# Whole-head loads of keys and values, and one load of the query weights, for the first element of a two-layer decode step

## The chip, the cores and the metric

The kernel runs on one core of one Trainium2 chip. The metric is the device time of one execution in microseconds, lower is better. The core has a matrix engine (PE; its weight loads are listed as PEld), a vector engine (DVE), an activation engine (ACT), a general engine (POOL), and a queue engine (SP) that issues nearly all transfers from the chip's memory. The transfers run on 16 DMA engines.

## What is computed

The reference is two passes of the same layer over four single-token elements (B = 4). In each pass an element attends over its cache and then goes through a gated feed-forward part. The caches and the weights are the same in both passes.

```python
def attention(x, k_cache, v_cache, wq, wo):        # x: 4 x 1 x 512
    q = (x @ wq).reshape(4, 1, 32, 128)            # 32 query heads
    k = repeat(k_cache, 4, axis=1)                 # caches: 4 x 8 heads x 4096 x 128
    v = repeat(v_cache, 4, axis=1)
    scores = einsum("bhqd,bhkd->bhqk", q, k) * 128 ** -0.5
    o = einsum("bhqk,bhkd->bhqd", softmax(scores), v)
    return o.reshape(4, 1, 4096) @ wo
def ffn(x, w_gate, w_up, w_down):                  # 512 -> 1792 -> 512
    return (gelu(x @ w_gate) * (x @ w_up)) @ w_down

for _ in range(2):
    x = x + attention(layernorm(x), k_cache, v_cache, wq, wo)
    x = x + ffn(layernorm(x), w_gate, w_up, w_down)
```

Everything is bf16. Since a softmax sum doesn't depend on the order of its 4096 positions, positions may be spread over partitions in any way, if keys and values of an element are spread alike.

## The kernel before

**Tiles.** The cache of one head is 4096 positions of 128 numbers, 1 MB. It is handled as two tiles (t = 0 and 1) of 512 KB: 128 partitions, and in each 16 positions one behind the other, which is 4 KB in a row. The 8 heads fall into two groups of 4, called `gx` and `gy`, so a group has 8 tiles of keys and 8 of values. Keys have room for 16 tiles (`KP`), one element's whole cache; values have a ring of 8 tiles (`slots`, `VRing`).

**One element's attention.** For a group, `q_first` (L921) projects the queries with `wq` (64 small matmuls on PE at L252) and corrects them for the layernorm on DVE (L923, L926, L248, L249). `q_build` spreads them into block weights `qb` (PE L324, DVE L331). Each key tile is turned in place by DVE (`turn`, L507, a stream transpose of 32x32 blocks). Then PE multiplies a turned tile with `qb` in 4 matmuls (`scores_of`, L557). The four heads of a group write to different groups of 32 output partitions, so that matmuls of different heads can run beside each other, while those of one head follow each other. `soft` takes the maximum (DVE L567), then the exponential (ACT L579); `soft_turn` (DVE L587), `soft_swap` (PE L609, ACT L612) and `soft_den`/`soft_recip` (PE L592, DVE L597) bring the probabilities into place. `vals.step(n)` then takes n value tiles, 16 matmuls each (PE L805); it ends with a scaling on DVE (L642) for each pair of heads that is complete. A value tile's place in the ring is free when its matmuls have run, and `ring.pump` then issues the next load into it.

**What sets the order.** The schedule is written out by hand: every engine takes its instructions in the order in which the program issues them. All large loads go through the one SP queue in program order. Up to eight loads are in flight; the ninth waits until the first has landed.

**The first element** (`attend_first`, L899 and on) has no earlier work to hide behind. SP issues, in this order: the half of `wq` that belongs to `gx` (2 MB), 8 key tiles of `gx`, the other half of `wq` (2 MB), 8 key tiles of `gy`, 8 value tiles of `gx`, 8 value tiles of `gy` (each into the place of a `gx` tile that has been used), and then the weights `wo`, `wg`, `wu`, `wd` (`load_rest`, L145 to L153), and the next element's keys. Keys are turned and scored by halves: all four heads at t = 0, then all four at t = 1.

Of the kernel before, what the change touches and what calls it, by code (L numbers as in the profile page):

```python
# [9 lines left out]
BF16 = mybir.dt.bfloat16  # L10
# [5 lines left out]
P = 128  # L16
# [8 lines left out]
GH = 4  # L25
CH = 16
V_SLOTS = 8
# [7 lines left out]
def kernel(  # L35
# [15 lines left out]
    _, Hkv, Sk, Dh = A_k_cache.shape  # L51
# [5 lines left out]
    KD = D // P  # L57
    KF = F // P
    C = Sk // P
    NT = C // CH  # L60
    assert NT == 2 and CH * QS == 512
    NG = Hkv // GH
    assert NG == 2
    HG = GH * rep
    NK = GH * BE
    W = 4 * QD
    TG = GH * NT
# [3 lines left out]
    wts = ctx.enter_context(tc.tile_pool(name="wts", bufs=1))  # L71
# [14 lines left out]

    dq = nc.sync

    wq_sb = [wts.tile([P, KD, HG * Dh], BF16, name=f"wq_sb{g}") for g in range(NG)]
    wo_sb = wts.tile([P, Hq, D], BF16, name="wo_sb")  # L90
    wg_sb = wts.tile([P, KD, F], BF16, name="wg_sb")
    wu_sb = wts.tile([P, KD, F], BF16, name="wu_sb")
    wd_sb = wts.tile([P, KF, D], BF16, name="wd_sb")
    KP = [[[wts.tile([P, 2, CH, Dh], BF16, name=f"kp{g}_{t}_{j}") for j in range(GH // 2)]
           for t in range(NT)] for g in range(NG)]
    slots = [wts.tile([P, CH, Dh], BF16, name=f"v_t{i}") for i in range(V_SLOTS)]
    wq_dram = A_wq.rearrange("(k p) n -> p k n", p=P)
    wo_dram = A_wo.rearrange("(i p) n -> p i n", p=P)

# [14 lines left out]
    qb = const.tile([P, W + NK * 2 * W], BF16, name="qb")  # L114
    cs_f = const.tile([P, 2, KF], FP32, name="cs_f")

    place = {(g * GH + s, t): (KP[g][t][s // 2], s % 2)
             for g in range(NG) for s in range(GH) for t in range(NT)}

    def k_tile(i, t):  # L120
        pair, n = place[i, t]
        return pair[:, n]

    def acc(shape, name, t=None):
        if t is None:
# [10 lines left out]
        return v.unsqueeze(1).broadcast_to([P, WIDE // n, n])  # L136

    def cache_tile(cache, b, kvh, t):
        return cache[b, kvh].rearrange("(t p c) d -> t p c d", t=NT, p=P)[t]

    def load_wq(g):
        n = HG * Dh
        dq.dma_start(out=wq_sb[g][:], in_=wq_dram[:, :, g * n:(g + 1) * n])

    def load_rest():  # L145
        n = Hq // 4
# [67 lines left out]
    class Norm:  # L214


        def __init__(self, st):
            ln = small.tile([P, 3, B], FP32, name="ln", tag="ln")
            self.mean, self.up, self.down = ln[:, 0, 1:2], ln[:, 1, 1:2], ln[:, 2, 1:2]
            self.ss, self.var, self.msq = ln[:, 0, :1], ln[:, 1, :1], ln[:, 2, :1]  # L220
            nc.vector.tensor_copy(out=ln[:, 0, :2], in_=st[:, 0])
# [33 lines left out]
    def q_proj(rhs, nb, g):  # L255
        w = nb if nb > 1 else WIDE
        q = acc([HG, w], "q")
        q_heads(q, rhs, nb, g, range(HG))
        return q
# [213 lines left out]
    class Keys:  # L473
# [4 lines left out]

        def tile(self, n):
            g, u = divmod(n, TG)  # L480
            t, s = divmod(u, GH)
            return self.groups[g] * GH + s, t

        def load(self, count):
            for _ in range(count):
                kvh, t = self.tile(self.nl)
                self.nl += 1
                dq.dma_start(out=k_tile(kvh, t), in_=cache_tile(A_k_cache, self.b, kvh, t))

        def load_pairs(self, count):  # L490
            for _ in range(count):
                kvh, t = self.tile(self.nl)
                (to, n), (other, m) = place[kvh, t], place[kvh + 1, t]
                if to is not other or (n, m) != (0, 1):
                    self.load(2)
                    continue
                self.nl += 2
                pair = A_k_cache[self.b, kvh:kvh + 2].rearrange("h (t p c) d -> t p h c d",
                                                                t=NT, p=P)
                dq.dma_start(out=to[:], in_=pair[t])  # L500

        def turn(self, count=1):
            for _ in range(count):
# [40 lines left out]
    singly = tuple((s,) for s in range(GH))  # L544
    last_alone = (tuple(range(GH - 1)), (GH - 1,))

    def scores(sc, g, t, runs=together):
        for run in runs:
            scores_of(sc, g, [(s, t) for s in run])

    def scores_of(sc, g, run):
        for be in range(BE):
            for s, t in run:
                n = s * BE + be
                w0 = n * 2 * W + (W if t == 0 else 0)
                kt = k_tile(g * GH + s, t).rearrange("p c (b j e) -> p c b j e", b=NB, e=2)
                nc.tensor.matmul(sc[s * QS:(s + 1) * QS], lhsT=qb[:, w0:w0 + 2 * W],  # L557
                                 rhs=kt[:, :, be // 2, :, be % 2],
                                 start=(t == 0 and be == 0),
                                 stop=(t == NT - 1 and be == BE - 1))  # L560
# [59 lines left out]
    def one(b):  # L620
        return [(g * GH + s, t) for g in first_groups[b] for s in range(GH) for t in range(NT)]

    def two(b):

        order = one(b)
        kept = order[len(order) - keep[b]:]
        rest = [u for u in reversed(order[:TG * (NG - 1)])]
        own = [u for u in reversed(order[TG * (NG - 1):]) if u not in kept]
        apart = [own.pop() for _ in range(2 if b else 0)][::-1]
        other = order[:TG]  # L630
        assert len(rest) == len(other)
        return list(reversed(kept)), own, other, apart
# [11 lines left out]
    class VRing:  # L644


        def __init__(self):
            self.free = [v[:] for v in slots]
            self.seq, self.at, self.ready = [], 0, {}

        def extend(self, layer, b, tiles):
# [2 lines left out]
        def pump(self, spare=None):  # L654
            free = self.free if spare is None else spare
            while self.at < len(self.seq) and free:
                key = self.seq[self.at]
                self.at += 1
                v = free.pop(0)
                dq.dma_start(out=v, in_=cache_tile(A_v_cache, *key[1:]))  # L660
                self.ready[key] = (v, spare is None)
# [214 lines left out]
    def dst1(b):  # L876
        last = one(b)[-1][0]
        return lambda k, n: (OL_bf[:] if k == last else OT_bf[:, k * rep:(k + n) * rep])
# [20 lines left out]
    def attend_first():  # L899

        b, (gx, gy) = 0, first_groups[0]
        prob1 = {}
        keys = Keys(b, (gx, gy))
        kept, own, other, _ = two(b)
        vals = Values(1, b, one(b), prob1, dst1(b), keeps=kept)
        ring.extend(1, b, one(b))
        load_wq(gx)
        keys.load(TG)
        load_wq(gy)
        keys.load(TG)  # L910
        ring.pump()
        make_identity(nc, ident_bf[:])
        build_consts()
        xT_ps = ps_sm.tile([P, KD, B], BF16, name="xT_ps", tag="sm")
        for k in range(KD):
            nc.tensor.transpose(xT_ps[:, k, :], x_bf[:B, k * P:(k + 1) * P], ident_bf[:B, :B])
        nc.vector.tensor_copy(out=xb[:, :, :B], in_=xT_ps[:])
        nc.vector.tensor_copy(out=XX.rearrange("p b k -> p k b"), in_=xT_ps[:])
        rstd1, mr1 = ln_scale(B, stats(0, B))

        def q_first(g):  # L921
            q = q_proj(lambda k: xb[:, k, :B + 1], B + 1, g)
            nc.vector.tensor_scalar(out=cs_q[:, g], in0=q[:, :, B], scalar1=float(D), scalar2=None,  # L923
                                    op0=ALU.mult)
            t = apart(wd_sb, [HG, B])
            nc.vector.tensor_tensor(out=t, in0=cols(cs_q[:, g], HG, B),  # L926
                                    in1=rows(mr1, HG, B), op=ALU.mult)
            center(q1_bf[:, g], q[:, :, :B], t, rstd1, B)

        q_first(gx)  # L930
        q_build(q1_bf[:, gx, :, b])
        keys.turn(4)
        sc1 = new_scores()
        scores(sc1, gx, 0, singly)
        keys.turn(4)
        scores(sc1, gx, 1, singly)
        p0 = soft(sc1)
        q_first(gy)
        soft_turn(p0)
        q_build(q1_bf[:, gy, :, b])  # L940
        pe, den = soft_swap(p0), soft_den(p0)
        keys.turn()
        prob1[gx] = (pe, soft_recip(den))
        keys.turn(3)
        vals.step(2)
        sc1 = new_scores()
        scores(sc1, gy, 0, last_alone)
        keys.turn(4)
        vals.step(3)
        scores(sc1, gy, 1, last_alone)  # L950
        vals.step(3)
        p0 = soft(sc1)
        soft_turn(p0)
        prob1[gy] = (soft_swap(p0), soft_recip(soft_den(p0)))
        vals.step(TG)
        assert vals.left() == 0
        load_rest()
        scr = Scratch()
        early = Early(b + 1, second_groups[b])
        proj = OutProj(o1(b), 1)  # L960
        for n, h in enumerate(pairs(one(b))):
            if n:
                busy(WARM, proj.bank[:, KD * WIDE:KD * WIDE + QS], ident_bf, start=False)
            proj.heads(h, hp)
        ring.extend(2, b, own)
        return proj.y, early, scr
# [391 lines left out]
    for b in range(B):  # L1358
        y = dense(b, y, prev, Scratch()) if b else dense_first(y, scr)
        gx, gy = second_groups[b]  # L1360
# [87 lines left out]
```

## Time and profile before

| | us |
|---|---|
| median of 3 runs | 270.62 (269.87 to 271.5) |
| the profiled execution, its own time | 273.38 |
| its span, first to last instruction | 271.6 |
| mean granted PE clock | 0.827 of full speed |
| DMA: moved 103.08 MB, mean over the span | 380 GB/s |
| busy: PE / DVE / ACT / POOL | 193.3 / 177.2 / 63.4 / 3.9 |
| chain that ended last: DMA / DVE / PE | 44% / 23% / 19% |

The page gives busy time by engine, a strip of 40 equal slices of the span, the chain of work that ended last (followed back from the last instruction to whatever released it), and the costliest groups of instructions. Queries of the trace give single instructions in order of time: start and duration in us, engine, line, operation, what is written and read, and in brackets how long the engine had stood idle and what ended that. Times count from the start of the span. The profiled execution's own time is 1.78 us longer than its span.

### The profile page before, as it was taken

What the parts mean: (1) busy time and instruction counts of PE and PEld (TensorE: products, weight loads), DVE (VectorE), ACT (ScalarE), POOL (GpSimd) and SP (SyncE); (2) the same over time, 40 slices, a digit from 0 to 9 for tenths busy, and PEclk for the clock granted to TensorE, in tenths of its full rate; (3) what the DMA queues carried; (4) which work ended last, traced back from release to release, by engine and by line L of the source; (5) the groups of instructions that cost most, each with busy time, mean ns of one, the idle gap of its engine ahead of it and who ended that gap; (6) DMA issues with size and microseconds to landing.
All of it is one profiled execution on the core that took longest, in us unless ns stands there. A gap on an engine that the chain in (4) does not pass through costs nothing.

```text
span 271.6 us, 9070 instructions
## 1 busy us (share of the span) xinstructions
PE 193.3 (71%) x4020; PEld 117.2 (43%) x4023; DVE 177.2 (65%) x435; ACT 63.4 (23%) x124; POOL 3.9 (1%) x10
## 2 busy tenths in 40 slices
PE   1395264655699796888769869587699685788783
PEld 1333133554475644445426245354372453443551
DVE  3493952151136999776748998756679987369843
ACT  1001001100405202024115320332144203164610
POOL 2000000000001000000000000000000000000010
PEclk9997559555599777959989989959989899599987
DMA  7999999999997999999999999999999999999910
GB/s 256 419 417 421 417 421 417 408 383 406 405 383 276 407 417 419 419 403 358 375 416 419 419 417 417 417 419 372 363 417 417 417 422 415 417 346 392 412 41 1
DMA packets 32574, 103.08 MB, mean 380 GB/s; under 512 B 2836, under 2 KB 8728, under 8 KB 32536
## 3 DMA queue, kind: packets, MB, share of 16 engines
q1 hardware_dynamic: 32512, 102.51, 95.0%
q8 instruction: 31, 0.51, 0.7%
q14 instruction: 7, 0.06, 0.0%
q10 hardware_dynamic: 24, 0.01, 0.0%
HBM read 102.50 MB, written 0.00 MB: 377 GB/s over the span
## 4 chain that ended last, share of the span: by engine, by line
DMA 44%; DVE 23%; PE 19%; SPq 9%; issue 3%; ACT 2%; DVEq 0%
DMA v_t<-in_A_v_cache_dram 19%; DMA kp<-in_A_k_cache_dram 17%; DVE kp L507 12%; PE sc L557 5%; DMA kp<-in_A_v_cache_dram 5%; SPq L148 4%; DMA wd_sb<-in_B_w_down_dram 4%; SPq L153 3%; PE ot L805 2%; PE so L738 2%; PE q L280 2%; DVE pe L587 1%; PE g L280 1%; PE y L252 1%; DVE q L286 1%
## 5 line engine op out<-in xcount | busy, mean ns | idle before, releaser
L507 DVE STREAM_TRANSPOSE kp<-kp 128x1024 f32<-128x1024 f32 x64 | 74.0, 1208 | 0.0
L557 PE MATMUL sc<-kp,qb 128*32 128x512 bf16 x512 | 66.2, 449 | 6.2 <-DVE kp L507 2.1
L805 PE MATMUL ot<-pe,v_t 128*128 128x32 bf16 x1120 | 35.5, 181 | 15.1 <-DMA v_t<-in_A_v_cache_dram 12.2
L805 PEld LDWEIGHTS <-v_t 128*128 128x128 bf16 x1120 | 33.0, 100 | 24.6 <-DMA v_t<-in_A_v_cache_dram 15.5
L557 PEld LDWEIGHTS <-qb 128*32 128x32 bf16 x512 | 22.3, 103 | 40.4 <-issue 23.0
L579 ACT ACTIVATE pe<-sc,nl 128x512 bf16<-128x512 f32 x8 | 5.5, 687 | 84.8 <-DVE pe L576 67.1
L609 PE MATMUL x<-pe,ident_bf 128*32 128x128 bf16 x192 | 5.6, 243 | 15.2 <-DVE pe L587 15.1
L746 DVE STREAM_TRANSPOSE so<-so 128x256 f32<-128x256 f32 (+1 forms) x19 | 11.1, 584 | 3.8 <-PE so L738 3.8
L609 PEld LDWEIGHTS <-ident_bf 128*32 128x32 bf16 x256 | 5.6, 106 | 18.4 <-issue 16.4
L738 PE MATMUL so<-v_t,pe 128*32 128x256 bf16 x192 | 9.3, 312 | 4.2 <-DMA v_t<-in_A_v_cache_dram 2.0
L567 DVE TENSOR_REDUCE pe<-sc 128x1 f32<-128x512 f32 x12 | 8.3, 690 | 6.0 <-PE sc L557 5.9
L252 PEld LDWEIGHTS <-wo_sb 128*128 128x128 bf16 x256 | 8.7, 104 | 6.3 <-DMA wo_sb<-in_A_wo_dram 5.4
L612 ACT CAST pe<-x 128x512 bf16<-128x512 f32 x12 | 7.0, 586 | 18.5 <-PE x L609 18.5
L738 PE MATMUL so<-v_t,pl 128*32 128x256 bf16 x192 | 9.9, 299 | 1.6 <-DMA v_t<-in_A_v_cache_dram 1.6
L252 PE MATMUL y<-OT_bf,wo_sb 128*128 128x32 bf16 x192 | 7.3, 190 | 5.1 <-DMA wo_sb<-in_A_wo_dram 4.9
L642 DVE TENSOR_TENSOR OT_bf<-ot,rden 128x8 bf16<-128x8 f32 (+1 forms) x20 | 3.0, 156 | 12.1 <-PE ot L805 12.0
L324 PE MATMUL qe<-q_bf,ident_bf 128*32 128x16 bf16 (+1 forms) x272 | 5.5, 175 | 7.6 <-DVE q_bf L306 4.8
L252 PE MATMUL q<-xb,wq_sb 128*128 128x5 bf16 (+1 forms) x192 | 5.7, 170 | 7.3 <-DMA wq_sb<-in_A_wq_dram 7.3
L587 DVE STREAM_TRANSPOSE pe<-pe 128x512 bf16<-128x512 bf16 x12 | 8.4, 699 | 3.4 <-ACT pe L579 3.4
L395 DVE TENSOR_TENSOR xb<-XX,y 128x4 bf16<-128x4 f32 (+1 forms) x9 | 1.6, 173 | 12.9 <-PE y L252 12.8
L376 PE MATMUL yr<-wo_sb,OT_bf 128*2 128x512 bf16 (+1 forms) x96 | 9.4, 453 | 0.0
L738 PEld LDWEIGHTS <-pe 128*32 128x32 bf16 x208 | 5.4, 105 | 9.0 <-issue 3.1
(153 smaller groups left out, 241.0 us busy)
## 6 DMA issues: line engine op xcount, KB each, us to landing
v_t<-in_A_v_cache_dram SPq DMA_DIRECT2D x97, 512.0 KB, 8.1
kp<-in_A_k_cache_dram SPq DMA_DIRECT2D x56, 512.0 KB, 10.0
wq_sb<-in_A_wq_dram SPq DMA_DIRECT2D x2, 2048.0 KB
wo_sb<-in_A_wo_dram SPq DMA_DIRECT2D x4, 1024.0 KB, 11.4
kp<-in_A_k_cache_dram SPq DMA_DIRECT2D x4, 1024.0 KB, 8.8
wq_sb<-in_A_v_cache_dram SPq DMA_DIRECT2D x3, 1024.0 KB, 12.7
wg_sb<-in_B_w_gate_dram SPq DMA_DIRECT2D x1, 1792.0 KB, 12.4
wu_sb<-in_B_w_up_dram SPq DMA_DIRECT2D x1, 1792.0 KB
```

The costliest lines, as they stand in the source:

```text
L148: dq.dma_start(out=wo_sb[:, i * n:(i + 1) * n], in_=wo_dram[:, i * n:(i + 1) * n])
L153: dq.dma_start(out=wd_sb[:, lo:hi], in_=wd_dram[:, lo:hi])
L252: nc.tensor.matmul(dst, lhsT=lhsT, rhs=rhs, start=first, stop=last, skip_group_check=True)
L376: nc.tensor.matmul(self.rows[j:j + x.shape[1]], lhsT=x, rhs=wo_sb[:, i], start=self.n < QD, stop=True, skip_group_check=True)
L507: nc.vector.transpose(out=words, in_=words)
L557: nc.tensor.matmul(sc[s * QS:(s + 1) * QS], lhsT=qb[:, w0:w0 + 2 * W], rhs=kt[:, :, be // 2, :, be % 2], start=(t == 0 and be == 0), stop= ...
L567: nc.vector.tensor_reduce(out=m, in_=sc.rearrange("p c j -> p (c j)"), axis=AX.X, op=ALU.min if norm else ALU.max)
L587: nc.vector.transpose(out=flat, in_=flat)
L609: nc.tensor.matmul(x[a * QS:(a + 1) * QS, s], lhsT=ident_bf[:, s * QS:(s + 1) * QS], rhs=pT[:, a], start=True, stop=True, skip_group_check ...
L738: nc.tensor.matmul(ps[d, :NW * QS], lhsT=x[:, w:w + NW].rearrange("p c h -> p (c h)"), rhs=v[:, i:i + NW, d], start=first and i == 0, stop ...
L746: nc.vector.transpose(out=flat, in_=flat)
L805: nc.tensor.matmul(self.ot[:, s % 2], lhsT=v[:, i, :], rhs=wide(pe[:, s, t * CH + i, :]), start=(done == 0 and i == 0), stop=(done == NT - ...
```

## The change

It touches the first element alone. A head's two tiles now lie beside each other, and which position goes to which partition is changed for the element's keys and values: a partition holds 32 positions in a row (8 KB) instead of two runs of 16 (4 KB each). So a head's keys, or its layer-1 values, come with one load of 1 MB. `wq` comes with one load of 4 MB, issued after the keys of two heads. Keys are turned, and scored, head by head. In group `gy` three heads are turned and scored together, then come 3 value tiles, and then the fourth head. The second pass's values of this element are still loaded by tiles of 4 KB rows, now 8 KB apart. Loads of the other elements keep their form.

```diff
-    wq_sb = [wts.tile([P, KD, HG * Dh], BF16, name=f"wq_sb{g}") for g in range(NG)]
+    wq_all = wts.tile([P, KD, NG, HG * Dh], BF16, name="wq_sb")
+    wq_sb = [wq_all[:, :, g] for g in range(NG)]
-    KP = [[[wts.tile([P, 2, CH, Dh], BF16, name=f"kp{g}_{t}_{j}") for j in range(GH // 2)]
-           for t in range(NT)] for g in range(NG)]
-    slots = [wts.tile([P, CH, Dh], BF16, name=f"v_t{i}") for i in range(V_SLOTS)]
+    KP = [[wts.tile([P, 2, NT, CH, Dh], BF16, name=f"kp{g}_{j}") for j in range(GH // 2)]
+          for g in range(NG)]
+    VP = [wts.tile([P, NT, CH, Dh], BF16, name=f"v_t{i}") for i in range(V_SLOTS // NT)]
+    slots = [v[:, t] for v in VP for t in range(NT)]
...
+    def load_head(cache, kvh, to):
+        dq.dma_start(out=to.rearrange("p t c d -> p (t c d)"),
+                     in_=cache[0, kvh].rearrange("(p r) d -> p (r d)", p=P))
+    def load_wq():
+        dq.dma_start(out=wq_all.rearrange("p k g n -> p k (g n)"), in_=wq_dram)
...
         # VRing.pump
+                if key[:2] == (1, 0):
+                    if len(free) < NT:
+                        return
+                    own = [free.pop(0) for _ in range(NT)]
...
+                    load_head(A_v_cache, key[2], VP[n // NT])
...
         # attend_first
-        load_wq(gx)
-        keys.load(TG)
-        load_wq(gy)
-        keys.load(TG)
+        keys.load_heads(GH // 2)
+        load_wq()
+        keys.load_heads(NG * GH - GH // 2)
...
         q_build(q1_bf[:, gx, :, b])
-        keys.turn(4)
         sc1 = new_scores()
-        scores(sc1, gx, 0, singly)
-        keys.turn(4)
-        scores(sc1, gx, 1, singly)
+        for s in range(GH):
+            keys.turn(NT)
+            for t in range(NT):
+                scores_of(sc1, gx, [(s, t)])
...
         vals.step(2)
         sc1 = new_scores()
-        scores(sc1, gy, 0, last_alone)
-        keys.turn(4)
+        keys.turn(2)
+        for t in range(NT):
+            scores_of(sc1, gy, [(s, t) for s in range(GH - 1)])
         vals.step(3)
-        scores(sc1, gy, 1, last_alone)
+        keys.turn(2)
+        for t in range(NT):
+            scores_of(sc1, gy, [(GH - 1, t)])
         vals.step(3)
         p0 = soft(sc1)
```

More of the change, by code (lines that the diff above doesn't have):

```diff
@@ L115 @@
     cs_f = const.tile([P, 2, KF], FP32, name="cs_f")
-    place = {(g * GH + s, t): (KP[g][t][s // 2], s % 2)
+    place = {(g * GH + s, t): (KP[g][s // 2], s % 2, t)
              for g in range(NG) for s in range(GH) for t in range(NT)}
     def k_tile(i, t):
-        pair, n = place[i, t]
-        return pair[:, n]
+        pair, n, half = place[i, t]
+        return pair[:, n, half]
     def acc(shape, name, t=None):
@@ L138, in cache_tile @@
     def cache_tile(cache, b, kvh, t):
+        if b == 0:
+            return cache[b, kvh].rearrange("(p t c) d -> t p c d", t=NT, p=P)[t]
         return cache[b, kvh].rearrange("(t p c) d -> t p c d", t=NT, p=P)[t]
-    def load_wq(g):
-        n = HG * Dh
-        dq.dma_start(out=wq_sb[g][:], in_=wq_dram[:, :, g * n:(g + 1) * n])
+    def load_head(cache, kvh, to):
[3 more added lines that the diff above has]
+        dq.dma_start(out=wq_all.rearrange("p k g n -> p k (g n)"), in_=wq_dram)
     def load_rest():
@@ L480, in tile, with load_heads @@
             g, u = divmod(n, TG)
-            t, s = divmod(u, GH)
+            if self.b == 0:
+                s, t = divmod(u, NT)
+            else:
+                t, s = divmod(u, GH)
             return self.groups[g] * GH + s, t
+        def load_heads(self, count):
+            for _ in range(count):
+                kvh, t = self.tile(self.nl)
+                self.nl += NT
+                pair, n, _t = place[kvh, t]
+                load_head(A_k_cache, kvh, pair[:, n])
         def load(self, count):
@@ L492, in load_pairs @@
                 kvh, t = self.tile(self.nl)
-                (to, n), (other, m) = place[kvh, t], place[kvh + 1, t]
-                if to is not other or (n, m) != (0, 1):
+                (to, n, half), (other, m, also) = place[kvh, t], place[kvh + 1, t]
+                if to is not other or (n, m) != (0, 1) or half != also:
                     self.load(2)
@@ L499, in load_pairs @@
                                                                 t=NT, p=P)
-                dq.dma_start(out=to[:], in_=pair[t])
+                dq.dma_start(out=to[:, :, half], in_=pair[t])
         def turn(self, count=1):
@@ L647, in __init__ @@
         def __init__(self):
-            self.free = [v[:] for v in slots]
+            self.free = list(slots)
             self.seq, self.at, self.ready = [], 0, {}
@@ L657, in pump @@
                 key = self.seq[self.at]
+                if key[:2] == (1, 0):
+                    if len(free) < NT:
+                        return
+                    own = [free.pop(0) for _ in range(NT)]
+                    n = [i for i, v in enumerate(slots) if v is own[0]][0]
+                    assert n % NT == 0 and own[1] is slots[n + 1]
+                    load_head(A_v_cache, key[2], VP[n // NT])
+                    for t in range(NT):
+                        assert self.seq[self.at] == key[:3] + (t,)
+                        self.at += 1
+                        self.ready[key[:3] + (t,)] = (own[t], spare is None)
+                    continue
                 self.at += 1
@@ L946, in attend_first @@
         sc1 = new_scores()
-        scores(sc1, gy, 0, last_alone)
-        keys.turn(4)
+        keys.turn(2)
+        for t in range(NT):
+            scores_of(sc1, gy, [(s, t) for s in range(GH - 1)])
         vals.step(3)
-        scores(sc1, gy, 1, last_alone)
+        keys.turn(2)
+        for t in range(NT):
+            scores_of(sc1, gy, [(GH - 1, t)])
         vals.step(3)
```

## The prediction

> **What bounds the kernel now.** I read the strip first: the DMA share is 9 in nearly every slice and 417 to 421 GB/s in slices 2 to 7, so the stream of loads sets the time as long as nothing makes it run dry. Then I read the chain that ended last, in order of time:
>
> ```profile
> 26.84 10.09 DMA v_t<-in_A_v_cache_dram
> 36.98 0.62 PE ot L805 x16
> 37.62 9.25 DMA v_t<-in_A_v_cache_dram
> 46.89 4.16 SPq L148
> ```
>
> In the first element the chain runs through value loads and touches PE once, where a ring place comes free. So there are two questions: does the stream get faster, and does it still never wait for a place. The instructions in order of time answer the second:
>
> ```profile
> 8.31 1.87 PE L252 MATMUL q<-xb,wq_sb 128*128 128x5 bf16 x64 [4.89 <-DMA wq_sb<-in_A_wq_dram]
> 11.80 9.12 DVE L507 STREAM_TRANSPOSE kp<-kp 128x1024 f32<-128x1024 f32 x8
> 22.04 0.69 DVE L567 TENSOR_REDUCE pe<-sc 128x1 f32<-128x512 f32 x1 [1.12 <-PE sc L557]
> 24.40 1.87 PE L252 MATMUL q<-xb,wq_sb 128*128 128x5 bf16 x64 [2.40 <-DMA wq_sb<-in_A_wq_dram]
> 27.99 1.22 DVE L507 STREAM_TRANSPOSE kp<-kp 128x1024 f32<-128x1024 f32 x1
> 29.28 7.94 DVE L507 STREAM_TRANSPOSE kp<-kp 128x1024 f32<-128x1024 f32 x7
> 35.76 0.61 PE L805 MATMUL ot<-pe,v_t 128*128 128x32 bf16 x16 [6.79 <-DMA v_t<-in_A_v_cache_dram]
> 37.52 1.93 PE L557 MATMUL sc<-kp,qb 128*32 128x512 bf16 x16
> 41.20 1.14 PE L557 MATMUL sc<-kp,qb 128*32 128x512 bf16 x16
> 45.06 0.68 DVE L567 TENSOR_REDUCE pe<-sc 128x1 f32<-128x512 f32 x1
> 57.17 1.17 PE L252 MATMUL y<-OT_bf,wo_sb 128*128 128x32 bf16 x32 [2.19 <-DMA wo_sb<-in_A_wo_dram]
> ```
>
> The first half of `wq` lands at 8.3, the first turn starts 3.49 later, and DVE turns back to back, 1.14 a tile. All 16 turns are over at 37.2. From 35.8 on PE waits for values; compute is ahead of the stream. The clock of PE comes from the stretches (columns: stretch, its length, busy time of PE, PEld, DVE, ACT, POOL, then clock, DMA share, GB/s):
>
> ```profile
> 22.00:24.00 2.00, 0.00 (x1) 0.00 (x0) 1.28 (x5) 0.48 (x1) 0.00 (x0) 0.96 1.03 422
> 24.00:26.00 2.00, 1.60 (x60) 1.60 (x61) 0.00 (x0) 0.61 (x3) 0.00 (x0) 0.50 1.02 420
> 40.00:42.00 2.00, 1.74 (x48) 1.22 (x44) 0.17 (x1) 0.00 (x0) 0.00 (x0) 0.77 1.04 424
> ```
>
> The clock fell to half at the end of the 22 to 24 stretch, with PE idle since 22.0, and came back within 40 to 42, after some 3 us of nearly unbroken matmuls. The two groups of 16 score matmuls above show the price: 1.93 at half clock, 1.14 at full.
>
> **The change, step by step.** Times below are of the profiled execution.
>
> *Query weights land late.* Today 2.10 MB have come by 8.31 and 8.39 MB by 24.40 (the two waits for `wq`). Afterwards `wq` ends at 6.29 MB (two heads, 2.10, and `wq`, 4.19). On the line between the two it lands at 19.0; the earliest is 8.31 + 4.19 MB at 418 GB/s = 18.3, the latest 24.40 less 2.10 MB at 418 = 19.4. Longer rows may help: a row takes 16 x 4096 / 418 = 157 ns at 4 KB, and 16 x 1024 / 386 = 42 ns for `wo` (1 KB rows, 386 GB/s from 56 to 60). Linearly 8 KB take 309 ns, 424 GB/s, which is 0.2 us less by 6.29 MB. At worst the rate is that of `wo`, 1.3 us more. I take 424, so 18.8.
>
> *The turns wait for it.* In the built order of the changed program DVE still takes the query's instructions and `qb` ahead of the first turn, so the first two heads lie landed and unturned. First turn: 18.8 + 3.49 = 22.3; eight turns end at 31.4; maximum 1.12 later, 32.5. PE starts these scores at half clock, as now (from 13.1 to 17.2 they came about 0.4 us apart, then faster); that costs nothing where the clock rises after 4 us as today, and up to 1.2 us where it takes nearly 7. I take 0.3: 32.8 against 22.04.
>
> *The second projection no longer waits.* `wq` is there, so PE projects `gy` at once, at 32.8, where it now waited 2.4 us. First `gy` turn 3.59 later (24.40 to 27.99): 36.4. The fifth and sixth turn end 5.83 and 6.96 after that: 42.2 and 43.4. Probabilities are there 4.67 after the projection's start, at 37.5 (24.40 to the end of the ACT copy at 29.07); two value tiles end at 38.5 (32 such matmuls took 1.04). So the fifth values load is issued at 38.5, in time.
>
> *The new wait.* Now three heads are scored before the next three value tiles. PE has been idle from 38.5 to 42.2, longer than the idle times before which the clock fell (22.0 to 23.9), so I cost these at half clock: 2 x 1.93, to 46.1. Two more value tiles (0.57 each, the rows at 42 to 44) end at 47.2 and free the second 1 MB place. The stream has run dry by then: the four `gx` heads and the fifth add up to 17.83 MB, which pass by 45.2 at today's rate. From issue to the first bytes after a dry spell takes about 1 us:
>
> ```profile
> 82.54 0.90 SPq L488 DMA_DIRECT2D kp<-in_A_k_cache_dram  x2
> ```
>
> With it the strip of that stretch shows no bytes until 83.5. So the sixth head flows from 48.2 to 50.7, **3.0 us of gap**. A place is now two tiles, so it also comes free one tile later than today.
>
> *And a second one.* DVE's order has the scaling of the first heads (L642) between the sixth and the seventh turn. So the fourth head's turns, which could have run from 43.4, wait for the value tiles: 47.2 + 0.2, two turns 2.27, scores 1.12: 50.8. The next value tile ends at 51.4 and frees the third place; the seventh head flows from 52.4 to 54.9, **1.7 us of gap**. The place for the eighth is free at 52.5, in time; it flows to 57.4. Behind these loads on SP stand `wo`, `wg`, `wu`, `wd` and the next keys: all come later. `wo` starts at 57.4; today 20.97 MB have passed at 52.7.
>
> *What is late next.* The maximum of `gy` comes at 52.6 (45.06 today), value tiles 4.42 later, eight of 0.57: 61.6. `wo`'s first quarter is used at 57.17 + 4.7 = 61.9. They nearly tie, so nothing more is lost, but there is no cover either. From there to 78.5 the chain is transfers back to back, and then a compute chain that begins with the last of them; nothing gives the time back.
>
> *What costs nothing.* 17 fewer issues on SP (0.33 each): SP is hidden, eight loads deep. Transposes, matmuls and bytes are the same. In the built program the waits after the first element point to the same producers. The second pass's values of this element (4.19 MB in 4 KB rows 8 KB apart) I cost at nothing; at `wo`'s rate 0.8 us.
>
> **Sum:** 57.4 - 52.7 = 4.7 us, less 0.1 for the gaps' three loads at 424: **+4.6**. On the profiled execution 273.38 + 4.6 = 278.0; the median lies 2.8 lower, and the step is the same there: 270.6 + 4.6 = **275.2**. Bounds: full clock in the three heads' scores 2 x 0.79 less, `wq` at its earliest 0.5 less: +2.5. Upwards: slow first scores 0.9, the fourth head's at half clock 0.9, 1.9 us instead of 1 to restart twice (as at the start: first issue 0.74, first bytes near 2.6) 1.8: +8.2.
>
> On the clock, the Trainium skill (TensorE: Matmul & The Clock Gate, Part 1) has a free-running window of about 3.4 us: an idle window halves the clock, a busy one restores it. The rows at 22 to 24 and 40 to 42 agree. By it the phase differs from run to run, so the 1.6 us may in part not be paid.
>
> **Rivals.**
> *Longer rows make the stream faster, and it never runs dry: faster.* For it: DMA is the bound, and the 1 KB rows are 8% slower than 4 KB rows. 20.97 MB take 50.2 us at 418 and 49.5 at 424: 0.7 less, 269.9; at 430, the line's limit, 1.4 less, 269.2. It decides only if the sixth head's place is free by 44.2 and the seventh's by 46.7; I have 47.2 and 51.4, and nothing in DVE's order lets the turns start before `wq`. The Trainium skill (DMA: Bandwidth & Descriptors, Bandwidth) advises loads of 1 MiB or more and counts some 2 us fixed per load; the trace disagrees for loads that overlap: value tiles of 512 KB came 1.2 us apart.
> *The gaps are mostly hidden: within 0.5%.* PE at full clock and an early `wq` leave +2.5; if a restart cost nothing beyond the wait, 2 us less, +0.5: 271.1. For it: I have its price from one dry spell alone. Against it: all three have to come together.
> *The stages slip further, so that compute leads:* if the first scores, the fourth head and the restart all go badly, +6.5 and more, 277.5 to 279.
> *It doesn't do what it says:* if an 8 KB row goes as two packets, the rate stays at 418 and the forecast moves by 0.2.
>
> **Chances.** Forecast, two gaps, 0.74; further slip 0.08 (with it slower: 0.82); hidden 0.10; faster stream without gaps 0.08. A measurement of this kernel can tell about 0.5%, 1.35 us. The range goes from the edge of the hidden case to the upper bound, 271.8 to 278.8; what lies outside are the last two, 0.18, and a little of the further slip.
>
> **What would show it.** Right: PE's first projection near 19, `gx`'s maximum near 33, two dips of GB/s between 45 and 53, the value loads waiting there on SP for value matmuls, `wo` used near 62. Wrong: a turn before the projection, no dip, or a dip at 82 that is shorter by what was lost here.

## The result, and the profile after

The changed kernel takes **286.47 us** (median of 6 runs, 284.43 to 287.22) against 270.27 us for the kernel before beside it (6 runs, 269.66 to 271.74). The ratio is 1.0561, with a 95% interval of 1.0523 to 1.0599. The forecast was 275.2 us: slower, as it came, but by 4.6 us and not by 16.

The profiled execution took 287.22 us, with a span of 285.4 us and a mean granted clock of 0.833. That of the kernel before lay about 3 us above its median, so I compare the two traces at milestones, not at their ends.

The strip of the page (40 slices of 7.1 us) shows where the stream of loads now runs dry. Slices 7 and 8 are the first element:

```profile
DMA  7999996799995999999999999999999999999000
GB/s 280 424 432 425 425 422 246 265 364 398 411 402 200 390 418 419 416 417 384 355 418 418 416 421 417 418 394 370 410 416 423 417 417 416 361 371 414 35 2 3
```

The same instructions of the first element as were shown of before, in order of time:

```profile
17.99 1.87 PE L259 MATMUL q<-xb,wq_sb 128*128 128x5 bf16 x64 [13.52 <-DMA wq_sb<-in_A_wq_dram]
21.47 9.12 DVE L524 STREAM_TRANSPOSE kp<-kp 128x1024 f32<-128x1024 f32 x8
31.71 0.69 DVE L584 TENSOR_REDUCE pe<-sc 128x1 f32<-128x512 f32 x1 [1.11 <-PE sc L574]
...
36.51 1.04 PE L834 MATMUL ot<-pe,v_t 128*128 128x32 bf16 x32 [0.84 <-DMA v_t<-in_A_v_cache_dram]
...
40.98 3.57 PE L574 MATMUL sc<-kp,qb 128*32 128x512 bf16 x22 [1.67 <-DVE kp L524]
...
46.93 3.41 PE L574 MATMUL sc<-kp,qb 128*32 128x512 bf16 x8 [0.98 <-DVE kp L524]
...
51.77 0.68 DVE L584 TENSOR_REDUCE pe<-sc 128x1 f32<-128x512 f32 x1
...
61.91 1.17 PE L259 MATMUL y<-OT_bf,wo_sb 128*128 128x32 bf16 x32 [2.14 <-DMA wo_sb<-in_A_wo_dram]
```

PE's first projection waits 13.5 us for the query weights, the turns come behind it, and everything up to `wo` is late: `gx`'s maximum by 9.7 us, `gy`'s by 6.7, the use of `wo` by 4.7. The stretches show the two dry spells (columns as before: last the clock, the DMA share, GB/s):

```profile
44.00:46.00 2.00, 1.95 (x52) 1.46 (x49) 0.44 (x2) 0.00 (x0) 0.00 (x0) 0.50 0.22 90
46.00:48.00 2.00, 1.07 (x3) 0.39 (x3) 2.00 (x2) 0.00 (x0) 0.00 (x0) 0.50 0.57 164
48.00:50.00 2.00, 2.00 (x6) 0.58 (x4) 0.00 (x1) 0.00 (x0) 0.00 (x0) 0.50 0.88 369
50.00:52.00 2.00, 1.65 (x50) 1.37 (x49) 0.31 (x2) 0.00 (x0) 0.00 (x0) 0.99 0.29 33
52.00:54.00 2.00, 0.00 (x0) 0.00 (x0) 1.04 (x5) 0.69 (x2) 0.00 (x0) 0.87 0.68 270
```

Against 426 GB/s, the mean of the 38 us ahead of them, 44 to 48 lacks (336 + 262) x 2 us = 1.20 MB, or 2.8 us, and 48 to 54 lacks (57 + 393 + 156) x 2 us = 1.21 MB, again 2.8 us. The sum of the element's input and its attention (`xb`, DVE L402, L395 before), with which its feed-forward part begins, comes at 71.74 instead of 66.36: **+5.4 us**. The last element's `xb` after its feed-forward part, written at the same line, comes at 248.21 instead of 242.56, +5.65. So far that is the forecast.

Then the rest is lost in one place. In the last element of the kernel before, DVE copies parked values into the space of `wq` (L530) without waiting, and the maximum follows:

```profile
246.79 1.28 DVE L530 TENSOR_SCALAR wq_sb<-park 128x512 int32<-128x512 int32 x2
247.98 0.68 DVE L567 TENSOR_REDUCE pe<-sc 128x1 f32<-128x512 f32 x1
```

The same two in the changed kernel, with the load that comes ahead of them on SP's queue:

```profile
250.48 1.34 SPq L705 DMA_DIRECT2D wq_sb<-in_A_v_cache_dram  x2
254.63 1.99 PE L574 MATMUL sc<-kp,qb 128*32 128x512 bf16 x32 [0.64 <-ACT qb L348]
261.60 1.29 DVE L547 TENSOR_SCALAR wq_sb<-park 128x512 int32<-128x512 int32 x2 [9.07 <-DMA wq_sb<-in_A_v_cache_dram]
262.81 0.68 DVE L584 TENSOR_REDUCE pe<-sc 128x1 f32<-128x512 f32 x1
264.28 0.78 ACT L596 ACTIVATE pe<-sc,nl,ln 128x512 bf16<-128x512 f32 x1 [9.70 <-DVE pe L593]
```

DVE stands idle for 9.07 us ahead of the copy. The scores have been there since 256.6 (254.63 + 1.99), but their maximum stands behind the copy on DVE, and ACT and PE stand behind the maximum. It comes 14.8 us late: 5.65 from the first element and 9.1 from here. The chain that ended last names the same step:

```profile
250.48 11.10 DMA wq_sb<-in_A_v_cache_dram
261.60 1.29 DVE wq_sb L547 x2
262.89 0.61 DVE pe L584
```

**Why the copy waits.** In the last element the weights' space is used again. ACT copies parked values into k = 0 of `gx`, DVE into k = 1 of `gx`; values are loaded by pairs into k = 2, 3 of `gx`, k = 0, 1 of `gy`, and k = 2, 3 of `gy`. With two tiles these places lie apart. The merged tile `[P, KD, NG, HG * Dh]` has its 4 KB runs in the order k0 gx, k0 gy, k1 gx, k1 gy, and so on. The load into k = 0, 1 of `gy` goes to runs 1 and 3, counted from 0, and run 2, between them, is the one that DVE fills. They share no byte; but from its first byte to its last, the load's part contains the copy's. The theory that I tested is that the waits which the program is built with go by that stretch, so that DVE waits for a load that doesn't concern it. The rivals were that merging costs something by itself, that one load instead of two does it, or that the lost time has its cause in the first element.

### The profile page after: what moved, and what is told of

It is laid out like the page before. It is cut to its first block, busy times and chain, and to the rows that moved or that the text cites. A ratio compares the mean times of both kernels' runs of the same rounds, so it can differ in the third digit from the quotient of the medians.

```text
span 285.4 us, 9050 instructions
## 1 busy us (share of the span) xinstructions
PE 198.5 (70%) x4020; PEld 120.7 (42%) x4023; DVE 177.6 (62%) x435; ACT 63.3 (22%) x124; POOL 3.9 (1%) x10
## 4 chain that ended last, share of the span: by engine, by line
DMA 41%; PE 25%; DVE 22%; SPq 5%; issue 3%; ACT 3%; DVEq 0%
DMA v_t<-in_A_v_cache_dram 16%; DVE kp L524 11%; DMA kp<-in_A_k_cache_dram 11%; PE sc L574 7%; DMA wq_sb<-in_A_wq_dram 6%; DMA wu_sb<-in_B_w_up_dram 5%; PE so L767 4%; DMA wq_sb<-in_A_v_cache_dram 4%; SPq L155 3%; PE ot L834 3%; PE q L259 2%; PE y L259 2%; PE g L287 1%; PE yr L383 1%; PE q L287 1%
## 5 line engine op out<-in xcount | busy, mean ns | idle before, releaser
L574 PE MATMUL sc<-kp,qb 128*32 128x512 bf16 x512 | 70.6, 447 | 9.3 <-DVE kp L524 5.4
L574 PEld LDWEIGHTS <-qb 128*32 128x32 bf16 x512 | 24.2, 103 | 45.2 <-issue 28.0
L834 PE MATMUL ot<-pe,v_t 128*128 128x32 bf16 x1120 | 34.3, 181 | 6.2 <-DMA v_t<-in_A_v_cache_dram 3.9
L259 PE MATMUL q<-xb,wq_sb 128*128 128x5 bf16 (+1 forms) x192 | 5.6, 170 | 13.5 <-DMA wq_sb<-in_A_wq_dram 13.5
L767 PE MATMUL so<-v_t,pe 128*32 128x256 bf16 x192 | 11.7, 385 | 2.2 <-DMA v_t<-in_A_v_cache_dram 1.4
L259 PEld LDWEIGHTS <-wq_sb 128*128 128x128 bf16 x192 | 5.2, 98 | 14.1 <-DMA wq_sb<-in_A_wq_dram 13.6
L383 PE MATMUL yr<-wo_sb,OT_bf 128*2 128x512 bf16 (+1 forms) x96 | 10.6, 512 | 0.0
L767 PEld LDWEIGHTS <-pe 128*32 128x32 bf16 x208 | 6.9, 130 | 8.6 <-issue 3.9
L402 DVE TENSOR_TENSOR xb<-XX,y 128x4 bf16<-128x4 f32 (+1 forms) x9 | 1.6, 173 | 13.5 <-PE y L259 13.3
```

The costliest lines, as they stand in the source:

```text
L259: nc.tensor.matmul(dst, lhsT=lhsT, rhs=rhs, start=first, stop=last, skip_group_check=True)
L383: nc.tensor.matmul(self.rows[j:j + x.shape[1]], lhsT=x, rhs=wo_sb[:, i], start=self.n < QD, stop=True, skip_group_check=True)
L767: nc.tensor.matmul(ps[d, :NW * QS], lhsT=x[:, w:w + NW].rearrange("p c h -> p (c h)"), rhs=v[:, i:i + NW, d], start=first and i == 0, stop ...
L834: nc.tensor.matmul(self.ot[:, s % 2], lhsT=v[:, i, :], rhs=wide(pe[:, s, t * CH + i, :]), start=(done == 0 and i == 0), stop=(done == NT - ...
```

## The experiments

Ratios are to the kernel before on the same chip, with 95% intervals.

**1. Two tiles and two loads, at the place of the one.** The rest is the changed kernel.

```diff
-    wq_all = wts.tile([P, KD, NG, HG * Dh], BF16, name="wq_sb")
+    wq_sb = [wts.tile([P, KD, HG * Dh], BF16, name=f"wq_sb{g}") for g in range(NG)]
...
-        load_wq()
+        load_wq(gx)
+        load_wq(gy)
```

> The changed kernel, but the query weights are two tiles again and come with two loads of 2 MB, one right behind the other at the place of the one load of 4 MB. Theory A (two separate causes: the first element is 5.4 us late at its end, as forecast, and in the last element DVE waits 9.1 us for a load that goes to another part of the merged tile of query weights): the wait of 9.1 us before the two copies back into the query weights' space is gone, the first element is as late as in the changed kernel (gy's maximum near 52, wo used near 62); 276 to 277.5 us. Theory B (the last element's load is simply late, because the whole stream slipped; the tile has nothing to do with it): the wait stays and the time is 285 to 287 us.

Measured: 271.83 us, ratio 1.0011 [0.9977, 1.0044]. The wait in the last element is gone, as expected, but so is nearly all of the first element's slip, and that I had not expected. The reason is in one line of this kernel's trace:

```profile
12.97 1.87 PE L259 MATMUL q<-xb,wq_sb 128*128 128x5 bf16 x64 [9.58 <-DMA wq_sb<-in_A_wq_dram]
```

The half for `gx` is there after 4.19 MB, not after 6.29 MB, and PE projects 5.0 us earlier. `gy`'s maximum comes at 46.60 instead of 51.77, and `xb` at 66.81, 0.45 behind the kernel before. Two tiles and two loads take away both costs at once, and this run doesn't part them.

**2. Merging the tile alone.** The kernel before with the merged tile; both loads, one for each group, stay where they were, and so does everything else.

```diff
-    wq_sb = [wts.tile([P, KD, HG * Dh], BF16, name=f"wq_sb{g}") for g in range(NG)]
+    wq_all = wts.tile([P, KD, NG, HG * Dh], BF16, name="wq_sb")
+    wq_sb = [wq_all[:, :, g] for g in range(NG)]
```

> The kernel before, with the query weights in one tile and nothing else changed: two loads of 2 MB at their old places, keys and values by tiles, old order. Theory A: the first element is as before (gy's maximum near 45, wo used near 57), and the last element has a wait of about 9 us on DVE; 279 to 281.5 us. Theory B: no such wait, 270 to 271 us.

Measured: 279.65 us, ratio 1.0295 [1.0244, 1.0345], some 8 us. The first element is that of the kernel before (`gy`'s maximum at 45.42, `xb` at 66.94), and the wait stands alone:

```profile
254.42 1.29 DVE L531 TENSOR_SCALAR wq_sb<-park 128x512 int32<-128x512 int32 x2 [8.05 <-DMA wq_sb<-in_A_v_cache_dram]
```

8.05 us of idle DVE, and 8 us of time: a declaration that changes no instruction and no byte in the first element costs more than the forecast's whole sum.

**3. The weights for `gx` first.** As 1, with the keys' first loads moved behind the first half of the weights.

```diff
-        keys.load_heads(GH // 2)
         load_wq(gx)
+        keys.load_heads(GH)
         load_wq(gy)
-        keys.load_heads(NG * GH - GH // 2)
+        keys.load_heads(GH)
```

> Two tiles of query weights; gx's half is loaded first, then the four heads of keys of gx in whole heads, gy's half, the four heads of gy; the rest (8 KB rows, values by whole heads, the new order of turns and scores) as in the changed kernel. Theory A with the late weights as the reason for the first element's loss: first projection near 8.3, gx's maximum near 22, no gap in the stream between 44 and 54; the rows of 8 KB let 18 MB pass some 0.7 us sooner; 269 to 271 us. Rival (the loss of the first element comes from the new order, three heads and then one, and from value places of two tiles, whenever the weights come): two gaps stay, some 3 us or more, 273 to 275 us.

Measured: 273.87 us, ratio 1.0091 [1.0057, 1.0125], a time that the rival gave, though with one dry spell and not two. The projection is as early as before (8.50), `gx`'s maximum is at 22.98, and still `gy`'s comes at 47.15 (45.06 before) and `xb` at 67.37. So the order of weights and keys isn't all. Values come by whole heads, so their first step starts at 36.63 instead of 35.76; 24 score matmuls at half clock (3.60 us) and the third and fourth value tile stand before the second place of 1 MB comes free; and the stream drops to 299 and 332 GB/s in 46 to 50. That is the forecast's mechanism, a place that comes free too late, at a smaller size. Of the 2.5 us (0.9%) the trace shows 1.0 at `xb`; I have no cause for the rest.

**4. One tile with the group outermost.** As 1, but both groups in one tile, one behind the other.

```diff
-    wq_sb = [wts.tile([P, KD, HG * Dh], BF16, name=f"wq_sb{g}") for g in range(NG)]
+    wq_all = wts.tile([P, NG, KD, HG * Dh], BF16, name="wq_sb")
+    wq_sb = [wq_all[:, g] for g in range(NG)]
```

> As the changed kernel, but in the one tile of query weights the group stands outermost, so that what belongs to one group lies in one stretch; two loads of 2 MB at the place of the one. If the false wait comes from two parts that lie interleaved in one tile (a part of gy spans from its first to its last byte over a part of gx): the wait is gone, as with two tiles, 276 to 277.5 us. If it comes from there being one tile at all: the wait of about 9 us stays, 285 to 287 us.

Measured: 273.14 us, ratio 1.0002 [0.9945, 1.0058], with no idle DVE ahead of the copy. One tile is not the cause; the interleaving in it is. The time lies below the 276 us and more that I expected, because here too the two loads took away the first element's loss (`xb` at 66.78).

**5. The changed kernel, with the late values placed otherwise.** Tile, load and first element stay as changed.

```diff
-    room = [[wq_sb[g][:, k] ... for k in range(KD)] for g in (gx, gy)]
-    pairs_of = [wq_sb[g][:, k:k + NT] ... for g, k in ((gx, NT), (gy, 0), (gy, NT))]
+    room = [[wq_sb[g][:, 0] ... for g in (gx, gy)]]
+    pairs_of = [v ... for v in (wq_sb[gx][:, NT:], wq_all[:, 1], wq_sb[gy][:, NT:])]
```

> The changed kernel with one tile and one load of 4 MB of query weights as it is; only the places of the last element's values within that tile are chosen otherwise, so that no part spans from first to last byte over another (the parked tile goes to gy's first quarter, and one head to the second quarter of both groups). Theory A: the DVE wait of 9.1 us in the last element is gone and nothing else; the first element stays as late as in the changed kernel (wo used near 62, two gaps): 275 to 277 us, 8 to 11 less than the changed kernel. Rival (most of the loss comes along with the late first element, for instance by slower loads later): 281 us or more.

Measured: 277.27 us, ratio 1.0169 [1.0073, 1.0265]. The wait is gone, the two dry spells stay (86 and 147 GB/s in 44 to 48, 8 GB/s in 50 to 52), and `xb` comes at 71.75. This is the first element's cost by itself, and the forecast's size, though the interval reaches from 2 to 7 us. The expectation puts the condition a little too strongly: the loads of k = 2, 3 of the two groups still interleave with each other; what no longer happens is that a load's stretch contains a place which the copies fill.

**6 and 8. Smaller places for the values.** Kernels 1 and 3, with the values loaded by tiles of 512 KB again (the branch for whole heads in `VRing.pump` is taken out), and with all four turns of `gy` ahead of the value tiles.

```diff
-        keys.turn(2)
+        keys.turn(4)
         for t in range(NT):
             scores_of(sc1, gy, [(s, t) for s in range(GH - 1)])
         vals.step(3)
-        keys.turn(2)
```

> Two tiles of query weights behind the first two heads, gx's half first (as in the first run); and the two other suspects undone: the values come by tiles of 512 KB, so that a place comes free one tile earlier, and the fourth head of gy is turned ahead of the value tiles instead of behind them. If these two make what is left of the gap (283 GB/s from 46 to 48 in the first run): no gap, gy's maximum near 45.5, wo used near 56.5; 269.5 to 271.5 us. Rival (the gap comes from the projection that is still 4.5 us late): the gap stays, as in the first run 271 to 272 us.

> As the run with small value places, but with gx's weights ahead of all keys. What is left of the change is then 8 KB rows for the first element's keys and turns and scores by whole heads. The stream is faster by 1.7% for 8 MB of keys, 0.3 us, and no gap is expected; PE is idle before gy's scores, so they may run at half clock, but behind values that come as tiles this has slack: 269.5 to 271 us, the same as before within what can be told. If the time is 272 us or more, the order by heads itself costs something that is not named yet.

Measured: on kernel 1, 271.53 us, ratio 1.0021 [0.9975, 1.0068]. The time alone fits both the expectation and its rival; the trace decides, for the dry spell is closed (406 GB/s and more in 44 to 50) and `xb` comes at 66.51. On kernel 3, 272.94 us, ratio 1.0061 [1.0008, 1.0113], above the 272 us from which on I had said that something unnamed costs time. Early weights and small places together thus bring nothing over the kernel before, and what the remaining 0.6% consists of stays open.

**7. PE kept busy.** Kernel 5, with eight more matmuls into the scores' place, which is overwritten, ahead of the three heads' scores.

```diff
         sc1 = new_scores()
+        busy(8, sc1.rearrange("p c j -> p (c j)"), wq_sb[gx][:, 0])
         keys.turn(2)
```

> As the run with the places moved, with 8 matmuls whose result is overwritten, put ahead of the score matmuls of the three heads of gy, where PE stood idle and its clock was at half. If the half clock stretches the path to the value places: the clock rises before or during these scores, the 22 score matmuls take 2.3 us instead of 3.6 and those of the fourth head 2.2 instead of 3.4; wo is used 1.5 to 2.5 us earlier than without; 273 to 275 us. Rival (DVE's turns set the pace, not PE): within 0.5 us of the run without.

Measured: 274.62 us, ratio 1.0122 [1.002, 1.0223]. The granted clock stays at 1.00 from 40 to 52, and both groups of scores run faster:

```profile
40.99 2.17 PE L574 MATMUL sc<-kp,qb 128*32 128x512 bf16 x22 [0.26 <-DVE kp L524]
...
45.48 2.15 PE L574 MATMUL sc<-kp,qb 128*32 128x512 bf16 x8 [1.01 <-DVE kp L524]
```

That is 2.17 instead of 3.57 and 2.15 instead of 3.44 us. `gy`'s maximum comes 2.7 us earlier than in 5 (49.06 and 51.76) and `xb` 2.2 us earlier (69.59); `wo` is first used 1.0 us earlier (60.07 and 61.11), less than I expected. So in these two traces the half clock is 2.2 us of the first element's 5.4. The measured times can't confirm it, since the intervals of 5 and 7 overlap. The other 3.2 remain where the weights come late and the places are large; no run parts these two in this kernel.

**9. The merged tile of 2, with the late values placed as in 5.**

> The kernel before with the query weights' tile merged into one (groups interleaved), loads at their old places, and the last element's values put into parts of that tile of which none spans another (k = 0 of both groups for the banked tiles; k = 2, 3 of gx, k = 1 of both, k = 2, 3 of gy for the pairs). Theory (the wait comes from spans that overlap, not from merging): no idle DVE ahead of the copy into the tile, last element as in the kernel before, 270.5 to 272.5 us, ratio 0.997 to 1.003. Rival (merging by itself costs, or the smaller number of banked places does): 274 us or more, as much of the 8 us of e2_merge_alone as belongs to it.

Measured: 271.37 us, ratio 0.9981 [0.9935, 1.0028]. The copy follows without a wait, where kernel 2 had 8.05 us:

```profile
247.88 1.28 DVE L531 TENSOR_SCALAR wq_sb<-park 128x512 int32<-128x512 int32 x2
```

Merging by itself costs nothing that can be told. In four comparisons (1, 4 and 5 against the changed kernel, 9 against 2) the copy waits where the load's stretch contains its place, and nowhere else. That is not yet the rule by which the waits are made, as three more lines of the changed kernel show:

```profile
248.89 1.93 ACT L552 COPY wq_sb<-park 128x1024 bf16<-128x1024 bf16 x2 [2.05 <-PE q L287]
249.53 0.38 SPq L705 DMA_DIRECT2D wq_sb<-in_A_v_cache_dram  x1
250.74 0.61 PE L287 MATMUL q<-wq_sb,xb 128*32 128x512 bf16 x8
```

A coarser rule, by the row k without the group, would fit the four comparisons as well. But ACT copies into run 0 (`gx`, k = 0) until 250.82, and the load into runs 1 and 3, which has k = 0 in common with it, is issued at 250.48 without waiting. And the stretch alone doesn't make a wait: the load issued at 249.53 goes to runs 4 and 6, and at 250.74 PE reads run 5 between them (`gy`, k = 2), which the program has behind that load. The load can't have landed by then, for in 1.2 us at 389 GB/s, the mean of 249.5 to 262, not half of its 1 MB passes. So DVE's copy inside a load's stretch waited, and PE's read inside another's did not; the exact rule stays open.

**10 and 11. The changed kernel and kernel 5 beside each other,** with no further edit, on one chip.

> The changed kernel itself, nothing edited, on the chip on which the next kernel runs too, so that the two can be subtracted. Theory (two causes that add): 285.5 to 287.5 us, and 8 to 9.5 us above the next kernel, which is the time that DVE stands idle for the load. Rival (the two causes are not all of it): the difference and the first element's 5.4 us leave 1.5 us or more over.

> The changed kernel with the last element's values in parts of which none spans another, as e5_places_moved. Theory: 276 to 278 us, 5 to 6 us above the kernel before, all of it from the first element. Rival: under 275 or over 279 us, so that the split between the two causes is another one than the trace's 5.4 and 9.1 us.

Measured: 285.99 us, ratio 1.051 [1.0433, 1.0587], and 278.89 us, ratio 1.0213 [1.0132, 1.0293]. Their quotient, 1.051 / 1.0213 = 1.029, is the cost of the wait; merging alone gave 1.0295. DVE stood idle for 8.12 us here. So the two causes add, and account for the whole within what can be told: 2.1% from the first element and 2.9% from the last one. By the ratios the wait is (0.0510 - 0.0213) x 271 = 8.0 us, by the plain medians 7.1, less than the 8 to 9.5 that I expected; each ratio is uncertain by 0.8%, so it can't be told more exactly whether it is 7, 8 or, as the idle time of the first trace has it, 9 us.

## Why the prediction was right on the direction and wrong on the size

**Query weights land late: right.** Forecast 18.8, seen 17.99, which is earlier than the 18.3 that I had given as the earliest: the stream ran at 429 GB/s from 6 to 26 us, and not at 418 to 424.

**The turns wait for it: right.** First turn 22.3, seen 21.47; `gx`'s maximum 32.8, seen 31.71. Each step kept its spacing, but for the 0.3 us for slow first scores: the maximum stood 1.11 us behind the last turn, as before. I had read a half clock from the spacing of the scores between 13.1 and 17.2; the granted clock of these stretches is 1.00, so what spaces them stays open.

**The second projection no longer waits: right.** It ran at 31.61, and the first `gy` turn at 35.08 (forecast 36.4).

**The two dry spells: right in place and cause, together 1 us too small.** Forecast 3.0 and 1.7 us; the stretches lack 2.8 and 2.8. The queue of SP spent 13.0 us waiting for value matmuls in that part. What I had mis-sized is the fourth head's eight scores: counted at full clock, with half clock as an upper bound of 0.9 more, they ran at half clock (3.41 instead of 2.15 us). The other traces with the same weights, loads and places of the first element bear out both (times in us; a dry spell is what the stretch lacks against the 426 GB/s that each has from 6 to 44):

| kernel | three heads' scores | fourth head's | lacking in 44 to 48 | in 48 to 54 | `xb` behind 66.36 |
|---|---|---|---|---|---|
| changed | 3.57 | 3.41 | 2.8 | 2.8 | 5.4 |
| 5 | 3.57 | 3.44 | 2.9 | 2.8 | 5.4 |
| 10 | 3.57 | 2.15 | 2.8 | 1.7 | 4.9 |
| 11 | 3.22 | 2.15 | 2.4 | 1.7 | 3.9 |
| 7 | 2.17 | 2.15 | 1.5 | 1.7 | 3.2 |

With the fourth head at full clock the second dry spell is the 1.7 us of the forecast; with the three heads at full clock the first falls to 1.5, where the lower bound had 3.0 - 1.6 = 1.4. And `xb` is late by about the sum of the two.

**What is late next: right.** `gy`'s maximum 52.6, seen 51.77; `wo` used at 61.9, seen 61.91; and nothing gave the time back up to 248 us. That `wo` meets the forecast so closely is luck, since the weights came 0.8 us earlier and the dry spells took 1 us more than forecast. The near tie with the value tiles wasn't there: these ended at 59.8, and PE waited 2.14 us for `wo`.

**Sum of the first element: +4.6, seen +5.4** in the first trace, 3.9 to 5.4 in the four that have it without kernel 7's extra matmuls, and 1.0169 and 1.0213 in kernels 5 and 11, which are 4.6 and 5.8 us. Kernel 5, at 277.27, lies inside the stated range, kernel 11, at 278.89, just above it. (The lower end of the range was to be 1.35 us above 270.6, which is 272.0 and not 271.8.)

**The step that failed** stands among "what costs nothing": "In the built program the waits after the first element point to the same producers." They didn't. The copy L547 had a new one, on the load L705. The step took the merged tile for another way of naming the same bytes. But the tile has a second life, in the last element, more than 230 us after the weights came; there its parts are written by two engines, and the order of the dimensions decides whether these parts lie apart. It cost some 8 us (7 to 9 by the reckonings above), nearly twice the sum, and accounts for most of the 11.3 us by which the forecast was short. The range went to +8.2 by the terms of the first element, and so held none of it.

**The rivals.** A faster stream: the rate did rise, see below, and moved nothing, since the places decide. The gaps hidden: no. Further slip: the half clock came, but the 11 us are not from there. The 2 us per load that I took from the Trainium skill (DMA: Bandwidth & Descriptors) stand there not under Bandwidth but in the anatomy of a DMA, for loads that the general engine issues; tiles that come 1.2 us apart on SP's queue show that no such time passes between overlapping loads, and not that the page is wrong. What I had no rival for is an edit to a tile's shape that adds a wait outside the stage which it was made for.

**On the clock,** the changed kernel ran twice with a trace, and shows by how much a single execution may differ. Up to 44.4 the instructions agree within about 0.3 us. Then the trace of run 10 has

```profile
46.87 2.15 PE L574 MATMUL sc<-kp,qb 128*32 128x512 bf16 x8 [1.00 <-DVE kp L524]
```

where the first trace has 3.41 us at 46.93: the clock was back to 1.00 in the 46 to 48 stretch of the one, and still 0.50 in that of the other. `gy`'s maximum differs by 1.3 us (50.45 and 51.77), and `xb` by 0.5. The Trainium skill (TensorE: Matmul & The Clock Gate, Part 1) says that the window by which activity is judged runs freely, so that the same kernel meets it in another phase each time; these two traces agree. In kernel 7 the extra matmuls ran from 37.36 to 40.42; the clock, at 0.58 and 0.56 in 36 to 38 and 38 to 40, was at 1.00 from 40 on, before the three heads' scores began. One reading in the prediction went too far: the row at 22 to 24 agrees only in part with the idle window of 3.4 us that it cites, since PE had been idle for no more than 1.9 us when its clock fell.

## What to carry to other kernels

Before a tile is merged, reshaped or reordered, look up every use of its space, late ones above all: a strided part that contains another part between its first and last byte may be taken for overlapping it, and an engine then waits for a transfer that it doesn't need. Put what is written separately into separate tiles, or make the dimension that parts them the outermost. And a larger load is paid for by whoever needs its first half; here two loads of 2 MB at the place of one of 4 MB brought `xb` of the first element from 71.74 to 66.81, nearly to where it had been.

## What the runs showed of the hardware

Longer rows went with a slightly faster stream: from 6 to 26 us, with keys by whole heads (8 KB rows), it ran at 423 to 429 GB/s in the changed kernel and in kernels 1, 5 and 6, and at 420 GB/s in 4 KB rows in the kernel before and in 2. From 36 to 44, while values came, kernel 1, with whole heads, had 426, kernel 6, with tiles of 512 KB (4 KB rows, 8 KB apart), 417, and the kernel before, with 4 KB rows one behind the other, 419. Rows and loads grew together in the change, so the runs don't say which of the two it is. In the time it doesn't show: the ratios of 1, 4 and 6, which have the longer rows without the two costs, lie between 1.000 and 1.002, and each interval holds 1. No version was clearly faster than the kernel before.
